# MLP weights loaded 512 columns at a time, four MLP units ahead of the k folds, tile 0 transposed on TensorE, tile 3 not centred first

## Chip, cores, metric

One core of a Trainium2 chip. The metric is device time in microseconds (us) of one execution; most executions of one kernel lie within 0.3%. Ratios of time come with a 95% interval. The profiled span is 1.7 us shorter than the time.

## The reference

`x` is 2048 tokens by 640. After a layer norm, two branches are added to `x`: a linear attention with 32 heads of 20, whose feature maps are softmaxes of `±(q W)` and `±(k W)`, and a gated MLP of width 1536.

```python
xn  = _layernorm(x)
qkv = xn @ wqkv                            # 640 -> 3 * 640
pq, pk = q @ w_phi, k @ w_phi              # per head, 20 x 20
phi = concat(softmax(p), softmax(-p))
o   = (phi_q @ (phi_k^T v)) / (phi_q . sum(phi_k))
out = x + o @ wo + (silu(xn @ w1) * (xn @ w3)) @ w2
```

## The kernel before, where it matters

The kernel lists its operations with what they read and write. A list scheduler inside it, with a model of durations and DMA landings, then puts them into one static order for each engine. A seed shakes the scheduler's choices up to 175 us of its own time.

Tokens come in 16 tiles of 128. The per-head 20x20 matrices are folded into `wqkv` first: a *fold* makes one fifth of the folded weight in 6 matmuls, from block-diagonal `w_phi` (`BDc`) and all five slices of transposed `wqkv` (`wqkT`; each slice is written by one DMA transpose, five for k, five for q). So even the first fold waits for the last slice. A *V tile* or *K tile* multiplies one token tile by the v weights or by the folded weight `Wkp`. An *MLP unit* is 10 matmuls of 512 columns: one chunk of 128 MLP columns for 512 tokens, so it needs tiles 0 to 3 normalised and transposed (`xnT`). An *eviction* is the copy by ACT or DVE that takes a result of TensorE out of its output memory (PS in the rows). *Warm-up matmuls* on constants fill TensorE where it has no work.

A *centred* tile has its mean removed early (`xc`), is transposed by TensorE into `xcT`, and its v tile (`v_first`) needs only that; the scale is applied at eviction. A tile that is not centred waits for the whole norm and takes `v_tile`, from `xnT`.

```python
CENTRED = {0: "ACT", 1: "ACT", 2: "ACT", 3: "DVE"}   # who makes the mean
# ...
TURNED = (0,)                                        # normalised tile transposed by DMA
SEED = 230
# ...
    def load_wT(which, e, level, after=()):          # a DMA transpose of one slice
        return turn(wqkT[:, which * DC + e:which * DC + e + 1, :],
                    A_wqkv[:, which * D + 128 * e:which * D + 128 * e + 128], level, True, after)
# ... the loads of the start; SyncE issues them in the scheduler's order
    n = len(P.all)
    load_w13(0, 384, lv - 4)                         # w1, then w3, columns 0 to 384
    for d in P.all[n:]:
        d.raw.add(chunk)                             # after a piece of wv
    first = [P.all[n]]                               # the w1 piece
    for e in range(DC):
        o = load_wT(1, e, lv - 9 - e, first)         # the k slices wait for it
        if e == 1:
            load(phi_s[:], phi_t, lv - 10.5, "SP", first)
    load_x(4, 8, lv - 19, "SP", [o])                 # waits for the last k slice
    # ...
    load_w13(384, 768, lv - 20)
    load_x(8, 12, lv - 21)
# ...
    for t in range(4):
        if t in CENTRED:
            xc_transpose(t, 6e4 - 10 * t + 15)
        if t in TURNED:
            turn(xnT[:, :, t * 128:(t + 1) * 128], x_tok[:, t, :], 2e6)
        else:
            xn_transpose(t, 3e4 - t if t in CENTRED else 6e4 - 10 * t + 15)
```

The softmax here doesn't subtract the row's maximum and nothing guards it: scores larger than these inputs give would overflow.

Of the kernel before, what the change touches and what calls it, by code (L numbers as in the profile page):

```python
# [4 lines left out]
ACT = mybir.ActivationFunctionType  # L5
# [63 lines left out]
class _Program:  # L69
# [366 lines left out]
    def emit(self, finish):  # L436
# [54 lines left out]
        for o in finish[-4:]:  # L491
            lists["SP"].append(("wait", o.sem[2], o.sem[1]))
        return lists
CENTRED = {0: "ACT", 1: "ACT", 2: "ACT", 3: "DVE"}
POOLED = ()
TURNED = (0,)
SEED = 230
TRIPLES = ((0, 3, 0, 60), (3, 3, 60, 60), (6, 3, 120, 60), (9, 3, 180, 60), (12, 3, 240, 60), (13, 3, 300, 20))


def bass_parallel_sum__linear_kernel_hedgehog__glu_gated_swiglu__prompt_kernel(
# [186 lines left out]
    def load(o, i, level=0.0, eng="SP", after=()):  # L688
        return P.dma(eng, lambda: queue[eng].dma_start(o, i), sb(o), sb(i), *pieces(o, 2 * o.shape[-1]), 0.45, level,  # L689
                     after)  # L690

    def turn(o, i, level=0.0, dram=False, after=()):
        d = P.dma("SP", lambda: nc.sync.dma_start_transpose(o, i), sb(o), sb(i), *pieces(o, 256),  # L693
                  1.31, level, after)
        d.extra = 1.0 if dram else 0.2
        return d
# [10 lines left out]
    def load_x(a, b, level, eng="SP", after=()):  # L707
        return load(x_tok[:, a:b, :], x_t[:, a:b, :], level, eng, after)

    def load_w1(a, b, level, eng="SP"):  # L710
        return load(w1_s[:, :, a:b], w1_t[:, :, a:b], level, eng)

    def load_w3(a, b, level, eng="SP"):
        return load(w3_s[:, :, a:b], w3_t[:, :, a:b], level, eng)

    def load_w13(a, b, level, eng="SP"):
        load_w1(a, b, level, eng)
        load_w3(a, b, level, eng)

    def load_wT(which, e, level, after=()):  # L720
        return turn(wqkT[:, which * DC + e:which * DC + e + 1, :],
                    A_wqkv[:, which * D + 128 * e:which * D + 128 * e + 128], level, True, after)
# [53 lines left out]
    def ln_apply(t, level):  # L776
        o, m, s, z = x_tok[:, t, :], mv[:, t, 0:1], mv[:, t, 4:5], mv[:, t, 6:7]
        ways = [w_op("DVE", "tensor_scalar", (o, o, m, s, ALU.subtract, ALU.mult), 0.35, 0.44)]
        if t in POOLED:
            ways = [w_op("POOL", "tensor_scalar", (o, o, m, s, ALU.subtract, ALU.mult), 2.5, 2.55)]  # L780
        if t >= 4:
            ways.append(w_act(o, o, ACT.Identity, D, s, z))
        add(ways, [o], [o, m, s, z] if t >= 4 else [o, m, s], None, level)

    def centre(t, level, by):
        o, i, z = xc[:, t, :], x_tok[:, t, :], mv[:, t, 6:7]
        if by == "BOTH":
            h, zb = D // 2, mv[:, t, 7:8]
            add([way("ACT", "activation", (junk[:, 0:h], i[:, 0:h], ACT.Copy), dict(scale=-1.0 / D, accum_out=z),
                     0.55, 0.58)], [junk[:, 0:h], z], [i[:, 0:h]], None, level)  # L790
            add([way("DVE", "tensor_scalar", (junk[:, h:D], i[:, h:D], -1.0 / D, None, ALU.mult, ALU.add),
                     dict(accum_out=zb), 0.48, 0.52)], [junk[:, h:D], zb], [i[:, h:D]], None, level)
            add([w_op("DVE", "tensor_scalar", (o, i, z, zb, ALU.add, ALU.add), 0.31, 0.41)], [o], [i, z, zb], None,
                level)
        elif by == "ACT":
            add([way("ACT", "activation", (junk[:], i, ACT.Copy), dict(scale=-1.0 / D, accum_out=z), 0.86, 0.87)],
                [junk[:], z], [i], None, level)
            add([w_op("DVE", "tensor_scalar", (o, i, z, None, ALU.add), 0.31, 0.41),
                 w_act(o, i, ACT.Identity, D, 1.0, z)], [o], [i, z], None, level)
        else:  # L800
            m = mv[:, t, 0:1]
            add([w_op("DVE", "tensor_scalar", (o, i, m, None, ALU.subtract), 0.31, 0.41)], [o], [i, m], None, level)

    def xc_transpose(t, level):
        n = 2 if t == 0 else 1
        u = P.begin(n, level)
        u.name = f"cT{t}"
        for dc in range(DC):
            l = xc[:, t, 128 * dc:128 * dc + 128]
            j, b = (0, dc) if n == 1 or dc < 3 else (1, dc - 3)  # L810

            def emit(l=l, j=j, b=b):
                a = (u.k + j) * 1024 + 128 * b
                return nc.tensor.transpose(PSb[:, a:a + 128], l, ident[:])
            P.mm(emit, [l, ident[:]], j, 0.056, 128)
        for j, a, b in ((0, 0, DC),) if n == 1 else ((0, 0, 3), (1, 3, DC)):
            def src(k, j=j, n=b - a):
                return PSb[:, (k + j) * 1024:(k + j) * 1024 + 128 * n].rearrange("p (c n) -> p c n", n=128)
            o = xcT[:, t, a:b, :]
            add([w_act(o, src, ACT.Copy, 128 * (b - a)), w_copy(o, src, 128 * (b - a), 2)], [o], [], [j], 1e6)  # L820
# [38 lines left out]
    def xn_transpose(t, level):  # L859
        u = P.begin(1, level)  # L860
        u.name = f"xT{t}"
        for dc in range(DC):
            l = x_tok[:, t, 128 * dc:128 * dc + 128]

            def emit(l=l, dc=dc):
                a = u.k * 1024 + 128 * dc
                return nc.tensor.transpose(PSb[:, a:a + 128], l, ident[:])
            P.mm(emit, [l, ident[:]], 0, 0.056, 128)

        def src(k):  # L870
            return PSb[:, k * 1024:k * 1024 + D].rearrange("p (c n) -> p c n", n=128)
        o = xnT[:, :, t * 128:(t + 1) * 128]
        add([w_act(o, src, ACT.Copy, D), w_copy(o, src, D, 2)], [o], [], [0], 1e6)
# [233 lines left out]
    lv = 9e5  # L1107
# [15 lines left out]
    load_wv(4, 5, lv - 3)  # L1123
    on_act(2.65, load_x, 3, 4)
    n = len(P.all)
    load_w13(0, 384, lv - 4)
    for d in P.all[n:]:
        d.raw.add(chunk)
    first = [P.all[n]]
    for e in range(DC):  # L1130
        o = load_wT(1, e, lv - 9 - e, first)
        if e == 1:
            load(phi_s[:], phi_t, lv - 10.5, "SP", first)
    load_x(4, 8, lv - 19, "SP", [o])
    n = len(P.all)
    load_w13(384, 768, lv - 20)
    load_x(8, 12, lv - 21)
    load_w13(768, 1152, lv - 22)
    load_x(12, 16, lv - 23)
    load_w13(1152, 1536, lv - 24)  # L1140
    for e in range(DC):
        load_wT(0, e, lv - 30 - e)
    for d in P.all[n:]:
# [9 lines left out]
    for t in range(4):  # L1153
        if t in CENTRED:
            centre(t, up - t, CENTRED[t])
        ln_apply(t, 1e5 - t)
# [7 lines that stand above are left out]
    for t in range(4, T, 2):  # L1164
# [14 lines left out]
    for t in range(2, 4):  # L1179
        (v_first if t in CENTRED else v_tile)(t, 6e4 - 10 * t)  # L1180
    for dc in range(DC):
# [33 lines left out]

    P.schedule({"PE": 0.8, "ACT": 1.12, "DVE": 0.93, "POOL": 0.8, "SP": 0.81}, filler, 12.0, SEED, 175.0)

# [60 lines left out]
```

## Time and profile before

| | before |
|---|---|
| time, median of 6 runs | 273.77 us (273.62 to 274.39) |
| profiled span, its execution's time | 272.9 us, 274.61 us |
| TensorE busy | 266.8 us, 98% |
| MLP matmuls recorded by the trace / weight loads for them | 465 / 480 |
| issue to landing of a 480 KB piece of w1 or w3, median | 6.8 us |

TensorE is the bound, so the question of each microsecond is whether TensorE does work at its pitch.

### The profile page before, as it was taken

The numbers are of one execution on the slowest core, as the hardware profiler recorded it, in microseconds if no ns is written. First come the engines' busy times: TensorE is split into PE (matmuls) and PEld (weight loads), VectorE is DVE, ScalarE is ACT, GpSimd is POOL, SyncE is SP. The second block draws the span as 40 slices with busy tenths as digits, with TensorE's granted clock in tenths as the row PEclk, the third lists the DMA queues.
The fourth block names the chain that finished last, engine by engine and source line by source line (L and its number), as shares of the span: only waits on it lengthen the run. The fifth ranks groups of instructions, "written<-read, shape, count | busy, mean of one in ns | idle before, by whom it ended". The sixth has DMA issues, their size and how long they took to land.

```text
span 272.9 us, 5057 instructions
## 1 busy us (share of the span) xinstructions
PE 266.8 (98%) x2076; PEld 158.9 (58%) x2095; DVE 181.4 (66%) x324; ACT 103.9 (38%) x194; POOL 61.0 (22%) x101
## 2 busy tenths in 40 slices
PE   8999999999999999999999999999999999999996
PEld 4747447777654446644544446677677774444774
DVE  5756999999998445469789978677661215666112
ACT  6637736777554541255493571010000002222000
POOL 4320643599999800000000000000000000000000
PEclk9999999999999999999999999999999999999999
DMA  7977999773000000712041131343332122000001
GB/s 221 191 98 241 342 221 157 116 168 112 0 0 2 0 0 4 228 62 32 19 50 24 26 49 24 82 113 78 96 98 79 67 73 73 0 0 0 26 24 48
DMA packets 41959, 22.14 MB, mean 81 GB/s; under 512 B 27728, under 2 KB 41936, under 8 KB 41936
## 3 DMA queue, kind: packets, MB, share of 16 engines
q1 hardware_dynamic: 41360, 21.17, 32.9%
q10 hardware_dynamic: 576, 0.66, 0.7%
q8 instruction: 16, 0.26, 0.4%
q14 instruction: 7, 0.06, 0.1%
HBM read 12.81 MB, written 2.62 MB: 57 GB/s over the span
## 4 chain that ended last, share of the span: by engine, by line
PE 82%; DMA 5%; POOL 4%; DVE 3%; SPq 2%; issue 2%; ACT 1%
PE PS L619 82%; POOL ekt L627 3%; SPq L693 2%; DMA w_s<-in_B_w_dram 2%; DMA wv<-in_A_wqkv_dram 1%; DMA wqkT<-in_A_wqkv_dram 1%; ACT EqT L627 1%; POOL mv L627 1%; DVE S L627 1%; DVE v L627 1%; DVE rS L627 1%; SPq L689 0%; DVE x_tok L627 0%; DVE Wqp L627 0%; DVE xres L627 0%
## 5 line engine op out<-in xcount | busy, mean ns | idle before, releaser
L619 PE MATMUL PS<-xnT,w_s 128*128 128x512 bf16 x465 | 105.1, 379 | 1.2 <-issue 0.5
L619 PEld LDWEIGHTS PS<-xnT,w_s 128*128 128x128 bf16 x480 | 46.3, 98 | 54.8 <-issue 0.3
L627 ACT ACTIVATE th<-PS 128x512 f32<-128x512 f32 x48 | 28.6, 597 | 71.2 <-PE PS L619 71.2
L619 PE MATMUL PS<-w_s,hT 128*128 128x320 bf16 (+2 forms) x384 | 55.0, 299 | 0.0
L627 DVE SCALAR_TENSOR_TENSOR t<-th,PS 128x512 bf16<-128x512 f32 x48 | 32.6, 682 | 26.2 <-ACT th L627 26.1
L619 PEld LDWEIGHTS PS<-w_s,hT 128*128 128x128 bf16 x384 | 37.1, 98 | 14.9
L627 DVE TENSOR_TENSOR xres<-PS,xres 128x640 bf16<-128x640 f32 (+2 forms) x17 | 13.4, 786 | 41.0 <-PE PS L619 41.0
L627 POOL TENSOR_TENSOR ekt<-ekt,rS 128x640 bf16<-128x640 bf16 x32 | 39.4, 1265 | 1.1 <-DVE rS L627 1.1
L627 DVE SCALAR_TENSOR_TENSOR hT<-t,PS 128x512 bf16<-128x512 bf16 x48 | 32.5, 680 | 1.1
L627 ACT ACTIVATE EqT<-PS 128x512 bf16<-128x512 f32 x40 | 22.0, 594 | 13.1 <-PE PS L619 13.0
L619 PE MATMUL PS<-wo_s,oT 128*128 128x320 bf16 (+2 forms) x160 | 24.5, 299 | 0.0
L627 DVE TENSOR_TENSOR prod<-PS,g_s 128x1280 bf16<-128x1280 f32 x16 | 23.9, 1491 | 0.5
L619 PE MATMUL PS<-Wkp,xnT 128*128 128x320 bf16 x160 | 23.9, 299 | 0.0
L627 ACT ACTIVATE ekt<-PS 128x640 bf16<-128x640 f32 x32 | 20.7, 699 | 7.4 <-PE PS L619 7.2
L619 PE MATMUL PS<-xnT,Wqp 128*128 128x512 bf16 x96 | 23.0, 379 | 0.4 <-issue 0.3
L627 DVE TENSOR_REDUCE S<-ekt 128x64 f32<-128x1280 bf16 x16 | 22.8, 1452 | 0.0
L627 ACT ACTIVATE e_s<-PS 128x64 f32<-128x64 f32 x32 | 9.1, 284 | 35.2 <-PE PS L619 34.8
L619 PEld LDWEIGHTS PS<-wo_s,oT 128*128 128x128 bf16 x160 | 15.7, 98 | 6.1
L619 PEld LDWEIGHTS PS<-Wkp,xnT 128*128 128x128 bf16 x160 | 15.5, 98 | 5.9 <-ACT Wkp L627 0.2
L619 PE MATMUL PS<-wv,xnT 128*128 128x320 bf16 x120 | 18.3, 299 | 0.0
L627 DVE BATCH_NORM_STATS2 bst<-x_tok 128x6 f32<-128x320 bf16 x32 | 14.3, 469 | 4.2 <-DMA x_tok<-in_A_x_dram 4.2
L619 PEld LDWEIGHTS PS<-xnT,Wqp 128*128 128x128 bf16 x100 | 9.3, 98 | 10.8
(67 smaller groups left out, 168.3 us busy)
## 6 DMA issues: line engine op xcount, KB each, us to landing
w_s<-in_B_w_dram SPq DMA_DIRECT2D x8, 480.0 KB, 6.8
xres<-in_A_x_dram SPq DMA_DIRECT2D x16, 160.0 KB, 2.2
out_dram<-xres SPq DMA_DIRECT2D x15, 160.0 KB, 1.8
x_tok<-in_A_x_dram SPq DMA_DIRECT2D x3, 640.0 KB, 7.6
w_s<-in_B_w_dram SPq DMA_DIRECT2D x1, 1920.0 KB, 9.2
wo_s<-in_A_wo_dram SPq DMA_DIRECT2D x1, 800.0 KB, 5.3
x_tok<-in_A_x_dram SPq DMA_DIRECT2D x2, 160.0 KB, 3.4
x_tok<-in_A_x_dram ACTq DMA_DIRECT2D x2, 160.0 KB, 3.7
```

What stands on the lines that cost most here:

```text
L619: return nc.tensor.matmul(o(u.k), l, r, start=start, stop=stop, skip_group_check=shared)
L627: return getattr(e, name)(*[at(a, u) for a in args], **{k: at(v, u) for k, v in kw.items()})
L693: d = P.dma("SP", lambda: nc.sync.dma_start_transpose(o, i), sb(o), sb(i), *pieces(o, 256), 1.31, level, after)
```

## The change

It means to take away the wait before the k folds: with 512 columns in the first load TensorE has four MLP units to do while the slices of `wqkv` come, and the scheduler is told that these land 2.4 us later than its model says. The other lines rearrange the start around this.

```diff
-CENTRED = {0: "ACT", 1: "ACT", 2: "ACT", 3: "DVE"}
+CENTRED = {0: "ACT", 1: "ACT", 2: "DVE"}
 POOLED = ()
-TURNED = (0,)
-SEED = 230
+TURNED = ()
+SEED = 1138
@@ loads
-    load_w13(0, 384, lv - 4)
+    load_w13(0, 512, lv - 4)
@@ k slices
         o = load_wT(1, e, lv - 9 - e, first)
+        o.extra = 2.4
@@ later loads
-    load_w13(384, 768, lv - 20)
+    load_w13(512, 1024, lv - 20)
     load_x(8, 12, lv - 21)
-    load_w13(768, 1152, lv - 22)
+    load_w13(1024, 1536, lv - 22)
     load_x(12, 16, lv - 23)
-    load_w13(1152, 1536, lv - 24)
```

## The prediction

> **What bounds the kernel now.** I read the page first (busy shares and the 40 slices), then TensorE's order of work in time, then who waits for whom, then the chain of waits, and last the issues of single DMAs in the first 30 us, because the diff touches only that stretch and the order that the kernel's own list scheduler makes of it.
>
> The page's first two parts, busy time (share, instructions) and busy tenths:
>
> ```profile
> PE 266.8 (98%) x2076; PEld 158.9 (58%) x2095; DVE 181.4 (66%) x324; ACT 103.9 (38%) x194; POOL 61.0 (22%) x101
> ...
> PE   8999999999999999999999999999999999999996
> ...
> PEclk9999999999999999999999999999999999999999
> ```
>
> TensorE (PE) is the bound, at full clock. A busy PE is not yet a PE at its pitch, so I count real work by start times. TensorE's rows in time (start, length, operation, count):
>
> ```profile
> 4.54 0.44 PE L814 MATMUL PS<-ident,xc 128*128 128x128 bf16 x5
> 4.82 0.45 PE L1098 MATMUL PS<-const-bfloat16-1.0 128*128 128x128 bf16 x5
> 5.57 0.99 PE L619 MATMUL PS<-wv,xcT 128*128 128x320 bf16 x6 [0.29 <-ACT xcT L627]
> ...
> 10.54 0.44 PE L814 MATMUL PS<-ident,xc 128*128 128x128 bf16 x5
> 10.82 1.00 PE L867 MATMUL PS<-ident,x_tok 128*128 128x128 bf16 x15
> 11.66 1.52 PE L619 MATMUL PS<-wv,xcT 128*128 128x320 bf16 x10
> 13.39 6.42 PE L619 MATMUL PS<-xnT,w_s 128*128 128x512 bf16 x29 [0.21 <-issue]
> 19.81 0.41 PE L619 MATMUL PS<-BDc,wqkT 128*128 128x80 bf16 x2
> 20.93 1.48 PE L619 MATMUL PS<-BDc,wqkT 128*128 128x140 bf16 x25 [0.71 <-DMA wqkT<-in_A_wqkv_dram]
> 22.25 5.60 PE L619 MATMUL PS<-Wkp,xnT 128*128 128x320 bf16 x40
> 27.90 12.90 PE L619 MATMUL PS<-xnT,w_s 128*128 128x512 bf16 x58
> ```
>
> The first useful matmul (transposes of centred token tile 0) starts at 4.54; then V of tiles 0 to 3, three MLP units (10 matmuls of 512 columns each), a pause of 0.71 for the last transposed slice of wqkv, the five folds, K of tiles 0 to 3, and MLP again at 27.90. Pitches from the same view: an MLP unit is 2.14 to 2.16 us (two start 2.16 apart at 74.52 and 76.68; twelve lie between 226.06 and 251.74, 25.68/12 = 2.14), a V or K tile 1.36 (40.63 to 41.99), five 128-column transposes 0.28 (10.54 to 10.82).
>
> Work between 4.54 and 27.90, in us: 35 transposes x 0.056 = 1.96; 4 V tiles x 1.36 = 5.44; 3 MLP units x 2.155 = 6.47; 30 fold matmuls at about 0.053 = 1.60; 4 K tiles x 1.36 = 5.44. Sum 20.9, in 23.36 us: **2.45 us of slack**, and this is all that the change can win there. It lies so: 1.1 before 10.54 (15 transposes and three V tiles, 4.9, in 6.0 us; warm-up matmuls 0.45, a wait of 0.29, small ones), 0.37 before the first MLP unit (10.54 to 13.39 is 2.85 for 20 transposes and one V tile, 2.48), 0.71 before the folds, 0.25 in small pieces.
>
> After 27.90 there is almost none. From 27.90 to 106.47 (the start of the kv sums) I count 18 MLP units, 24 V and K tiles, 5 Q units of 1.08 and 30 fold matmuls: 38.8 + 32.6 + 5.4 + 1.6 = 78.4 of 78.57 us. The end, 226.06 on, is matmuls at pitch to 270.39 and a fixed tail of addition and store, 2.5 us. TensorE's waits, all of them above 0.2 us in sum:
>
> ```profile
> PE PS L619 <- issue: 0.8, 5, 0.2
> PE PS L1098 <- PEq L1263: 0.8, 1, 0.8
> PE PS L619 <- DMA wqkT<-in_A_wqkv_dram: 0.7, 1, 0.7
> PE PS L619 <- ACT xcT L627: 0.3, 1, 0.3
> ```
>
> The long waits of the other engines and POOL's full slices 7 to 13 cost nothing: no row of TensorE names them.
>
> The start of the chain of waits shows why the folds come at 20.93:
>
> ```profile
> 5.16 5.61 DMA w_s<-in_B_w_dram
> 10.77 0.02 issue
> 10.79 1.17 SPq L693
> ...
> 17.27 3.53 DMA wqkT<-in_A_wqkv_dram
> ```
>
> SyncE starts the five DMA transposes of wqkv when the first w1 piece has landed (10.77), issues them one by one at 1.2 to 2.0 us each, with the small phi load between, and the last lands at 20.80.
>
> **What the Trainium skill says.** (1) "TensorE: Matmul & The Clock Gate", section "Wait — 56ns, not 53.3ns?": warm matmuls run at N / 2.4 GHz plus about 2.5 ns, 55.6 ns at 128 columns and 215.7 at 512. The trace agrees: 15 transposes in 0.84 us are 56 ns each, and an MLP unit of ten is 2.14 to 2.16 us. (2) "VectorE: DVE Perf Modes", section "The three transpose paths": TensorE transposes 128x128 in 390 ns into PSUM, the DMA in 1309 ns. In this kernel, pipelined, five TensorE transposes take 0.28 us plus an eviction of 0.49 (DVE) or 0.70 (ACT), while tile 0's DMA transpose was issued at 6.30 and took 6.6 us to land. (3) "DMA: Bandwidth & Descriptors", section "Bandwidth": larger transfers come nearer the peak, at least 1 MiB being advised. The loads grow from 480 to 640 KB, so I give this little; the trace moves 334 to 355 GB/s between 24 and 30 us already.
>
> **The change part by part.**
> *Tile 0 on TensorE.* Adds 5 transposes (0.28 us) and an eviction; removes a DMA transpose, 1.30 us on SyncE's queue and a landing at 6.30 + 6.6 = 12.9. This landing stands right at the end of V3 (11.66 + 1.36 = 13.0), so I suspect it behind the 0.37 before the first MLP unit. Without it that unit can start when the TensorE transposes are evicted: those of tiles 1 to 3 were all out at 12.35.
> *Tile 3 not centred.* Removes 5 transposes (0.28), the centring (0.38) and an eviction (0.49) on DVE. TensorE's sum of work is unchanged: 35 transposes either way. But V3 now needs the normalised, transposed tile like the MLP, so 1.36 us of work that filled 11.66 to 13.02 is no longer early. Before the first MLP unit there are 35 x 0.056 + 3 x 1.36 = 6.0 us of work; with 1.1 slack TensorE would be through at 11.7, and must wait for the last eviction, at about 12.2. V3 then goes anywhere later. Slack before the first MLP unit: 12.2 - 4.54 - 6.0 = 1.6, against 1.1 + 0.37 = 1.5. Loss 0.1 to 0.2.
> *Tile 2 centred by its mean from DVE.* Takes 0.74 + 0.19 off ACT and waits for two statistics and an aggregate (0.44 + 0.48 + 0.21 = 1.1), so its centred form is some 0.2 later; V1 covers that.
> *Loads of 512 columns.* w1 lands when 0.164 MB more has passed: at about 340 GB/s 0.5 us later, 11.25; w3, issued at 5.62 and landed 6.6 later by the list of single issues, near 12.2, comes at about 13.1. The second half of the first unit needs w3 1.08 after its start: 13.3. Just in time. The transposes of wqkv start 0.5 later, but no transpose of tile 0 stands before them; the last lands near 21.1.
> *Four units ahead of the folds.* The units run 12.2 to 20.8; with V3 (1.36) TensorE has work to 22.2, past 21.1. The 0.71 is gone. Folds and K take 7.0, so MLP resumes near 29.2. It then needs columns 512 to 1024. Before, that stretch's w1 and w3 were issued at 21.23 and about 21.8 and took 5.4 and 6.4, landing at 26.6 and 28.2; with 0.16 and 0.33 MB more and a start 0.3 later, 27.4 and 29.5, needed at 29.2 and 30.3. No wait expected.
> *Seed and the model's 2.4 us extra for those landings.* They move no work, only the order up to 175 us. Gaps from mode switches (five of 0.16 in the rows above) and evictions may change by 0.3 either way.
> Sum: -0.71 + 0.15 + 0 = about -0.55; 273.8 becomes 273.2.
>
> **The rivals.**
> *The new wait takes the old one's place:* w1 or w3 late by more than reckoned holds the first unit, or columns 512 to 1024 hold the unit after K. For it: margins of 0.2 to 1.8 us. Against: the pauses would be under 1 us, and V3 or another unit can be put in. Time 273.6 to 274.5.
> *The start fills better than I think:* ACT and DVE lose tile 3's early steps, the tiles are out by 11.7, and most of the 2.45 goes. Against: the input of tile 3 and its statistics (aggregated at 9.35 to 9.56, power on POOL to 10.60, scaled by 11.1) do not move. Time 272.0 to 272.6.
> *The folds were not worth waiting for at all:* the pause vanishes but the new seed gives the 0.5 back between 106 and 167 us, where softmax steps on DVE and ACT gate the token units. Time 273.5 to 274.
> A wait of many us would need the order to be badly off, and nothing in a stretch with 78.4 of 78.57 us filled suggests it.
>
> **Range and chances.** Predicted 273.2; 272.1 to 274.4 covers all three rivals. Two per cent is 5.5 us, over twice the slack that the change can touch (2.45), so faster by that is all but excluded; slower by that needs a stall that nothing shows. Faster 0.02, within 0.96, slower 0.02.
>
> **What would show it right or wrong.** Right: no wait of TensorE for wqkT; 40 MLP matmuls between V and the folds; folds beginning at 21 to 22.3; K of tiles 0 to 3 ending some 1.6 us later than 27.85 with one unit more done; the first MLP unit at 12 to 12.6 with no DMA wait; 78.5 us at pitch after. Wrong: a row of TensorE waiting for w_s (loads too big), for x_tok or xnT before 13 us for over 1 us (tile 3 too late), or a rise of the waits for DVE after 106 us (seed).

## More of the kernel before

The prediction shows TensorE's rows of the start. One line that I passed over belongs beside them, from the page's list of groups (count, then busy time and mean of one, then idle time before):

```profile
L619 PE MATMUL PS<-xnT,w_s 128*128 128x512 bf16 x465 | 105.1, 379 | 1.2 <-issue 0.5
L619 PEld LDWEIGHTS PS<-xnT,w_s 128*128 128x128 bf16 x480 | 46.3, 98 | 54.8 <-issue 0.3
```

There are 480 weight loads and 465 matmuls: 15 records of matmuls are missing. Where the missing one is the first of a row, the row shows 9 or 29 matmuls and seems to start 0.216 us late, behind a gap.

## The result, and the profile after

After: 273.35 us, median of 6 runs (273.20 to 274.27), against 273.77; ratio 0.9988, interval 0.9971 to 1.0005: the same, with a lean to faster. A ratio compares the means, so it is not quite the ratio of the medians quoted. Executions over 1.5% slower than the fastest of the same kernel are left out of the means.

The profiled span fell from 272.9 to 271.7. That is 1.2 us, more than the 0.42 of the medians, because the profiled execution of before was a slow one (274.61, above all six timed runs). The trace of before shows more to explain than there is.

TensorE's rows of the start of the kernel after:

```profile
4.63 0.74 PE L814 MATMUL PS<-ident,xc 128*128 128x128 bf16 x5
5.17 0.60 PE L1098 MATMUL PS<-const-bfloat16-1.0 128*128 128x128 bf16 x5
...
10.92 1.29 PE L867 MATMUL PS<-ident,x_tok 128*128 128x128 bf16 x20
12.05 1.52 PE L619 MATMUL PS<-wv,xnT 128*128 128x320 bf16 x10
13.40 8.80 PE L619 MATMUL PS<-xnT,w_s 128*128 128x512 bf16 x40
22.04 1.82 PE L619 MATMUL PS<-BDc,wqkT 128*128 128x140 bf16 x30
23.70 5.67 PE L619 MATMUL PS<-Wkp,xnT 128*128 128x320 bf16 x40
29.21 13.11 PE L619 MATMUL PS<-xnT,w_s 128*128 128x512 bf16 x60
```

All 40 matmuls of the four units are there, the folds follow at 22.04 with nothing between, and MLP resumes at 29.21. TensorE waits for nothing that the view of waits names, but its first instruction:

```profile
PE PS L1098 <- PEq L1263: 0.8, 1, 0.8
```

SyncE's issues in the kernel after (start, time on the queue) show when the slices come:

```profile
11.73 3.00 SPq L693 DMA_TRANSPOSE wqkT<-in_A_wqkv_dram  x2
...
15.40 3.83 SPq L693 DMA_TRANSPOSE wqkT<-in_A_wqkv_dram  x3
20.93 0.37 SPq L689 DMA_DIRECT2D x_tok<-in_A_x_dram  x1
```

The load of x at 20.93 waits for the last slice, so its start tells the landing: 20.9, no earlier than before (20.8), and 1.1 before TensorE reaches the folds.

For all traces I split the time at the V of tile 4, which every order puts behind K of tiles 0 to 3. The **start** is that moment less 2.158 us for each MLP unit already done (twelve units lie in 25.90 us, 224.68 to 250.58, in the trace after, where all 120 are recorded). The **rest** is the beginning of the last addition less the start. Before: V of tile 4 at 40.63 with 9 units done, so the start is 21.22 (with 2.157, as I used it below), and the last addition at 270.42 makes the rest 249.20. After: 42.16 with 10 units, 20.59, and 269.25, 248.66. So 0.6 us of the trace's difference are in the start and 0.5 in the rest.

One place of the rest is visible: the second and third q fold. Before took 0.90 us for these 12 matmuls (the next row starts at 66.30), as the second half of the second fold waited for the eviction of the first fold on DVE; after took 0.63 (66.92 to 67.55). Before:

```profile
65.28 0.48 DVE L627 CAST Wqp<-PS 128x320 bf16<-128x320 f32 x1
65.40 1.06 PE L619 MATMUL PS<-BDc,wqkT 128*128 128x140 bf16 x12
65.81 0.47 PEld L619 LDWEIGHTS PS<-BDc,wqkT 128*128 128x128 bf16 x9 [0.25 <-DVE Wqp L627]
```

### The profile page after: what moved, and what is told of

It reads as the page before. It is cut to its first block, busy times and chain, and to the rows that moved or that the text cites. A ratio compares the mean times of both kernels' runs of the same rounds, so it can differ in the third digit from the quotient of the medians.

```text
span 271.7 us, 5074 instructions
## 1 busy us (share of the span) xinstructions
PE 268.3 (99%) x2098; PEld 159.4 (59%) x2098; DVE 182.5 (67%) x325; ACT 101.8 (37%) x190; POOL 60.8 (22%) x101
## 4 chain that ended last, share of the span: by engine, by line
PE 99%; DVE 0%; issue 0%
PE PS L619 96%; PE PS L1098 2%; PE PS L867 0%; PE PS L814 0%; DVE xres L627 0%
## 5 line engine op out<-in xcount | busy, mean ns | idle before, releaser
L619 PE MATMUL PS<-xnT,w_s 128*128 128x512 bf16 x480 | 106.6, 379 | 0.0
L627 ACT ACTIVATE ekt<-PS 128x640 bf16<-128x640 f32 x32 | 20.8, 701 | 9.0 <-PE PS L619 8.8
L619 PE MATMUL PS<-wv,xnT 128*128 128x320 bf16 x130 | 19.8, 299 | 0.0
```

What stands on the lines that cost most here:

```text
L619: return nc.tensor.matmul(o(u.k), l, r, start=start, stop=stop, skip_group_check=shared)
L627: return getattr(e, name)(*[at(a, u) for a in args], **{k: at(v, u) for k, v in kw.items()})
```

## The experiments

Each kernel in 6 executions (5 rounds and the profiled one), compared with the kernel before on the same chip. The landing is that of the last k slice, read from SyncE's next load. The start and the rest are as defined above. These columns come from one profiled execution each.

| run | median us | ratio (95%) | landing | folds from | waits for wqkT | start | rest |
|---|---|---|---|---|---|---|---|
| before, first trace | 273.77 | 1 | 20.8 | 19.65 | 0.71 | 21.22 | 249.20 |
| a1_same | 274.04 | 0.9994 (0.998 to 1.0009) | 19.1 | 19.84 | 0 | 20.51 | 249.07 |
| a4_seed | 274.71 | 1.0015 (1.0002 to 1.0028) | 21.0 | 20.24 | 0.45 | 21.56 | 248.81 |
| b4_noextra | 274.10 | 0.9991 (0.9978 to 1.0003) | 20.1 | 19.90 | 0 | 20.46 | 248.73 |
| a3_tiles | 275.56 | 1.0054 (1.0036 to 1.0071) | 19.3 | 18.84 | 0.18 | 21.88 | 249.26 |
| after, first trace | 273.35 | 0.9988 (0.9971 to 1.0005) | 20.9 | 22.04 | 0 | 20.59 | 248.66 |
| c1_after | 273.72 | 0.9988 (0.9971 to 1.0006) | 21.2 | 21.91 | 0 | 20.46 | 248.66 |
| c2_latehalf | 274.00 | 1.0004 (0.998 to 1.0028) | 20.6 | 20.00 | 0.34 | 21.05 | 248.89 |
| d1_before_late | 275.06 | 1.004 (1.0015 to 1.0064) | 21.6 | 20.25 | 0.88 | 22.00 | 249.08 |
| d2_after_late | 274.55 | 1.0022 (1.0002 to 1.0042) | 22.0 | 22.74 | 0 | 21.28 | 249.45 |
| a2_loads | 274.98 | 1.0036 (1.0016 to 1.0056) | 20.5 | 21.08 | 0 | 21.63 | 248.90 |
| b1_allbutseed | 275.32 | 1.005 (1.0031 to 1.0069) | 19.5 | 21.15 | 0 | 21.80 | 248.81 |
| b2_turn0 | 274.92 | 1.0038 (1.0011 to 1.0065) | 21.0 | 22.63 | 0 | 21.18 | 248.74 |
| c4_afterfold | 273.68 | 0.9997 (0.9975 to 1.0018) | 19.3 | 21.80 | 0 | 20.35 | 248.73 |

The theory going in: the gain is the wait of 0.71, less a small loss at the start. The rivals: the seed's other order after 40 us makes it, or it is chance.

**a1_same.** No edit: the kernel before a second time.

> The kernel before, unchanged, run as if it were a new one: how far apart are two readings of the same program? My theory (the gain of 0.4 us is the removed wait for wqkT of 0.7, less what the start loses) expects a ratio of 1.000 within 0.001 and a second trace with the same wait for wqkT, 0.5 to 0.9 us, before the folds. The rival (the 0.4 us is the spread of the runs) expects two readings of one program to differ by 0.4 us or more.

The ratio is 1 within its interval, as both expected of a mean, but the wait is not there. TensorE's rows of this trace:

```profile
12.00 1.52 PE L619 MATMUL PS<-wv,xcT 128*128 128x320 bf16 x10
13.58 6.42 PE L619 MATMUL PS<-xnT,w_s 128*128 128x512 bf16 x29
19.84 1.86 PE L619 MATMUL PS<-BDc,wqkT 128*128 128x140 bf16 x30
21.54 5.60 PE L619 MATMUL PS<-Wkp,xnT 128*128 128x320 bf16 x40
```

The slices landed at 19.1, 1.7 us earlier than in the first trace, and the folds ran through. Of this, 1.1 was there when the slices set out: SyncE starts them when the first w1 piece has landed, at 10.79 in the first trace and at 9.73 here. One program in two executions: a start of 21.22 and one of 20.51. This half of my theory fell: the 0.71 was this execution's, not the kernel's.

**a4_seed.** The kernel before with `SEED = 1138`.

> The kernel before with the new seed alone. Its order is that of before up to the folds and differs after 30 us. My theory: the wait for wqkT stays at 0.5 to 0.9 us and the time at 273.6 to 274.0, ratio 0.999 to 1.001. The rival (the new order after 40 us makes the gain): the time falls to about 273.3, ratio 0.998 to 0.999, with the wait for wqkT still there.

Neither: it is slower, ratio 1.0015 (interval from 1.0002). The rest is 0.3 shorter than before's, as the rival wanted, but the seed also moved tile 0's DMA transpose behind the first slice of `wqkv` on SyncE's queue (issued at 11.02 instead of 6.30), and the first MLP unit waited for it:

```profile
13.99 6.42 PE L619 MATMUL PS<-xnT,w_s 128*128 128x512 bf16 x29 [0.33 <-DMA xnT<-x_tok]
21.11 1.57 PE L619 MATMUL PS<-BDc,wqkT 128*128 128x140 bf16 x25 [0.45 <-DMA wqkT<-in_A_wqkv_dram]
```

Here the DMA transpose of tile 0 is seen on the path, by name.

**b4_noextra.** The kernel after less one line:

```diff
         o = load_wT(1, e, lv - 9 - e, first)
-        o.extra = 2.4
```

> The kernel after without the 2.4 us that its scheduler adds to the landings of the transposed slices: the loads stay at 512 columns, but only three MLP units stand ahead of the first folds and the fourth comes between folds. My theory: TensorE waits again for wqkT, 0.5 to 1.3 us in sum, and the time is 273.8 to 274.5, ratio to before 1.000 to 1.003. The rival (seed or loads make the gain): as after, 273.3, ratio 0.998 to 0.999.

The order was as described: three units, three folds, the fourth unit, two folds. The wait did not come, and the ratio is that of after:

```profile
19.90 1.12 PE L619 MATMUL PS<-BDc,wqkT 128*128 128x140 bf16 x18
20.86 2.32 PE L619 MATMUL PS<-xnT,w_s 128*128 128x512 bf16 x9
23.02 0.79 PE L619 MATMUL PS<-BDc,wqkT 128*128 128x140 bf16 x12
```

My theory's number missed. The slices landed near 20.1, about when the first fold needed the last of them. So the place of the fourth unit alone is worth nothing measurable in a run where the slices are on time.

**a3_tiles.** The first two lines of the diff alone (`CENTRED`, `TURNED`).

> The kernel before with the tile part alone (tile 0 transposed on TensorE, tile 2 centred by DVE's mean, tile 3 not centred); loads of 384 columns, old seed. The scheduler then sets two MLP units ahead of the folds and the third behind them. My theory: TensorE reaches the folds near 18 us and waits there until wqkT lands at about 20, 1.5 to 2.5 us, so 275.0 to 276.0, ratio 1.004 to 1.008. A rival (the start matters little, since work moves freely) expects under 0.5 us of loss, ratio below 1.002.

The time fits, the reason doesn't: the wait for wqkT was 0.18. The loss lies ahead of the first unit, which starts at 14.5:

```profile
9.54 0.98 PE L1098 MATMUL PS<-const-bfloat16-1.0 128*128 128x128 bf16 x14
...
13.15 1.53 PE L619 MATMUL PS<-wv,xnT 128*128 128x320 bf16 x10 [0.42 <-DVE xnT L627]
```

With tile 3 no longer centred TensorE ran short of work, 14 warm-up matmuls filled in, and V of tile 3 waited for its transposed tile.

From here the theory was: the start of after is no better than before's good start, but cannot become before's bad one, since the fourth unit covers a late landing; and the rest is about 0.4 shorter.

**c1_after.** The kernel after again.

> The kernel after, unchanged, a second reading on another chip. By the traces so far, the time up to the V of tile 4 less 2.157 us for each MLP unit done by then is 21.22 and 20.51 for two traces of before and 20.59 for after; the rest is 249.20 and 249.07 for before and 248.66 for after. My revised theory: the rest is smaller by 0.4 us in every trace with the new seed, and the start is no better than before's good trace, but cannot have before's bad one, since the fourth unit covers a landing of wqkT up to about 22 us. So again a ratio of 0.997 to 0.999, a start of 20.4 to 20.8, a rest of 248.6 to 248.9, and no wait of TensorE for wqkT. The rival (the first comparison was chance): ratio 0.999 to 1.001 and a rest of 249 or more.

As expected on every count: ratio 0.9988, start 20.46, rest 248.66, no wait for wqkT although the slices landed at 21.2, later than in any trace of before with its own loads. The two readings together (their mean, the half-width of 0.0017 divided by the root of 2) give 0.9988 with an interval of about 0.9976 to 1.0000. Each reading alone includes 1.

**c2_latehalf.** The kernel before, whose scheduler changes to the new seed at 45 us:

```diff
         while left:
+            if seed is not None and seed > 0 and free["PE"] > 45.0:
+                rng, seed = random.Random(1138), -1
             best = None
```

> The kernel before with its own order up to 45 us of the scheduler's time and the new seed from there on; loads, tiles and the start untouched. My revised theory: the rest after the V of tile 4 falls from 249.1 to 248.6 to 248.8, the ratio is 0.998 to 0.9995, and the start has before's spread (20.5 to 21.3). The rival (the rest differs for another reason than the later order, for instance the loads): rest 249.0 to 249.3, ratio 1.000.

The trace's rest fell by 0.2 to 0.3, to 248.89 (just above what I expected), and the q folds no longer wait (0.63 for the 12 matmuls), but the timed ratio, 1.0004 with an interval of ±0.0024, can't show a gain of this size. The same program start as before gave a third value of the wait, 0.34, at a landing of 20.6. It also shows a second gap, ahead of the first unit:

```profile
13.74 6.42 PE L621 MATMUL PS<-xnT,w_s 128*128 128x512 bf16 x29 [0.54 <-issue]
```

With the missing record the unit starts at 13.53, 0.48 after V of tile 3 is through (13.05); tile 0's DMA transpose landed at 13.1 (issued at 6.52, 6.6 to landing). The landing accounts for the beginning of this gap; what held TensorE for the rest of it the trace does not name.

**d1_before_late, d2_after_late.** The same line in before and after makes the k slices wait for the w3 piece instead of w1:

```diff
-    first = [P.all[n]]
+    first = [P.all[n + 1]]
```

> The kernel before with the transposed loads of wqkv started when the first w3 piece has landed instead of the first w1 piece, so some 1.4 us later (w3 landed 1.4 after w1 in the trace of before); TensorE's order is the same up to the V of tile 4. My theory: before has no cover, so the wait for wqkT before the folds grows to 1.5 to 2.2 us and the time by 0.8 to 1.6 us, ratio 1.003 to 1.006. The rival (the wait is absorbed elsewhere or not on the path): ratio below 1.002.

> The same delay in the kernel after: the transposed loads of wqkv start when the first w3 piece of 512 columns has landed, some 1.5 to 1.9 us later, with TensorE's order unchanged through the folds. wqkT landed at 20.9 in the trace of after and is needed at 22.04, so my theory lets the fourth unit absorb 1.1 us of the delay: a wait for wqkT of 0.3 to 0.9 us and a time 0.3 to 1.0 above that of after, about equal to before, ratio 0.999 to 1.002. The rival (no cover): it loses the full 1.5 or more, ratio 1.003 or more.

The delay brings before waits of 0.18 and 0.70 (0.88; I had expected 1.5 or more) and 1.1 us of time:

```profile
20.79 0.22 PE L619 MATMUL PS<-BDc,wqkT 128*128 128x140 bf16 x1 [0.18 <-DMA wqkT<-in_A_wqkv_dram]
21.71 1.48 PE L619 MATMUL PS<-BDc,wqkT 128*128 128x140 bf16 x25 [0.70 <-DMA wqkT<-in_A_wqkv_dram]
```

In after the slices landed latest of all traces, 22.0, and no wait followed, where I had expected 0.3 to 0.9:

```profile
14.32 8.58 PE L619 MATMUL PS<-xnT,w_s 128*128 128x512 bf16 x39
22.74 1.82 PE L619 MATMUL PS<-BDc,wqkT 128*128 128x140 bf16 x30
```

So the cover is shown in the traces: TensorE reached the folds 0.7 later than in after, but even at after's 22.04 the last slice would have been in. In the times it is not clear of noise, as the intervals of d1 and d2 overlap. What I had not expected is that d2 still lost time without this wait (ratio 1.0022, just above my range). In its trace TensorE waited 0.40 for the centred tile 2 ahead of 9.15, so that everything behind came later, and the rest is 249.45 with another order after 45 us, in which an MLP unit at 142.43 waits 0.47 for an eviction on DVE. Neither is a wait for wqkT. Whether the delayed transposes have any part in them stays open.

**a2_loads.** The load lines and the 2.4 us alone, on the kernel before.

> The kernel before with the loads of 512 columns and the scheduler's 2.4 us alone; tile 0 still transposed by DMA, tile 3 still centred, old seed. Its scheduler puts three units, then four of five folds, a fourth unit and the last fold. My theory: the DMA transpose of tile 0 stands behind 1.3 MB of weights instead of 0.98, so the first MLP unit waits for it, 0.4 to 1.0 us, and the time up to the V of tile 4 less the units done is 21.2 to 21.9; the rest 249.0 to 249.3; ratio 1.001 to 1.004. The rival (the loads and the fourth unit carry the gain by themselves): ratio 0.997 to 0.999.

Ratio and start came in as my theory had them, and the rival fell. The wait, however, is put down to another:

```profile
13.57 0.44 PE L867 MATMUL PS<-ident,x_tok 128*128 128x128 bf16 x5
14.82 6.42 PE L619 MATMUL PS<-xnT,w_s 128*128 128x512 bf16 x29 [0.81 <-DVE xnT L627]
```

The DMA transpose of tile 0 (issued at 6.59, 6.7 to landing) was in at 13.2. The scheduler, presumably reckoning with a late landing, had put one tile's TensorE transposes behind V of tile 3, and their eviction (14.05 to 14.54 on DVE) held the unit. So this order cost more than a wait for the DMA transpose would have.

**b1_allbutseed.** The kernel after with `SEED = 230`.

> The kernel after with the old seed. The old seed puts the transposes of tiles 0 to 3 in another order: V of tile 2 is left in front of the transposes of tiles 1 to 3, and TensorE runs 14 warm-up matmuls and waits for tile 3. My theory: the first MLP unit starts near 14.5 (a gap of 0.4 to 0.8 us before V of tile 3, as in the run of the tile part alone), start 21.2 to 21.8, rest 248.7 to 249.3, ratio 1.000 to 1.003. The rival (the seed matters only after 40 us): start 20.4 to 20.8, ratio 0.999 to 1.0005.

As my theory had it for the trace (14 warm-up matmuls again, 0.43 before V of tile 3, start 21.80), with a loss above its range, 1.005. The seed is no ornament: with these tiles it decides whether the start fills. The rest, 248.81 with the old seed, also shows that the shorter rest does not belong to the number 1138.

**b2_turn0.** The kernel after with `TURNED = (0,)`.

> The kernel after with tile 0 transposed by DMA again. My theory: that transpose stands behind the two loads of 640 KB and lands at 13.5 to 14.2, so the first MLP unit waits for it by 0.3 to 0.9 us; start 20.9 to 21.5, rest 248.6 to 248.9, ratio 1.000 to 1.002. The rival (the DMA transpose was never on the path): start as after, 20.4 to 20.8, ratio 0.998 to 0.999.

```profile
11.83 1.53 PE L619 MATMUL PS<-wv,xnT 128*128 128x320 bf16 x10
14.22 8.58 PE L619 MATMUL PS<-xnT,w_s 128*128 128x512 bf16 x39 [0.86 <-ACT v L627]
```

One record is missing here (39, and 22.63 less 40 matmuls of 0.2158 is 14.00), so the unit started at 14.0, 0.8 after V of tile 3 was through (11.83 + 1.36 = 13.19). The profile names the eviction of v on ACT, but that ended at 14.11, after the start; the DMA transpose landed at 13.9 (issued at 11.18, 2.7 to landing). That transpose is the release that fits. The start lost 0.6 to 0.7 against after. The time lost 0.5% against it (1.0038 / 0.9988), more than I had expected and twice what this trace shows: its execution was the fastest of six, three of which took 274.1 to 274.4 and three 275.4 to 276.0. What the slower three lost has no trace.

**c4_afterfold.** The kernel after, the q folds' evictions at a higher level (the scheduler's priority):

```diff
-            add([w_act(...), w_copy(o, src, 320)], [o], [], [q], 1e6)
+            add([w_act(...), w_copy(o, src, 320)], [o], [], [q], 1e6 if which else 2e6)
```

> An attempt to beat both: the kernel after with the evictions of the q folds given a higher level in the scheduler, so that no fold waits for one (in before one of them waited 0.27 us; in after none does). If nothing is left to win there, as I think: start 20.4 to 20.8, rest 248.6 to 248.9, ratio 0.997 to 0.9995, as after. The rival (evictions of the folds still cost something): rest below 248.4.

Start 20.35, rest 248.73: as after, and the ratio 0.9997, a little above what I expected, is not told apart from after's. No gain is seen there; no version beats after. Its slices landed at 19.3 with after's loads.

## Why the prediction was right

The time predicted was 273.2, the time measured 273.35 and, in the second reading, 273.72, inside 272.1 to 274.4; the class is the same, as given 0.96. Point by point:

- **"about -0.55", sum:** measured -0.42 in the medians, -0.26 in the second reading. The size fits, its make-up only in part: the wait was on average worth less than I took, the loss ahead of the first unit is not there, and a gain in the rest that I had not forecast is. So the hit on the size is in part luck.
- **"-0.71", the wait for wqkT:** gone in all traces of after (landings 20.9 and 21.2, folds at 22.04 and 21.91). But the term was mis-sized: with before's own start the wait was 0.71, 0 and 0.34 in three traces, 0.35 on average. (Counted from the first fold to K of tile 0, which leaves modelled ends of matmuls out, it is 2.60, 1.70 and 2.07 against 1.66 in after: the wait cost 0.9, 0 and 0.4.) I read one execution as the kernel. What the change removes is an exposure to a landing that moves by 1.7 us between executions.
- **"Loss 0.1 to 0.2" ahead of the first unit:** not shown. I had the unit at 12.2 with V of tile 3 afterwards; it came at 13.40, right behind V of tile 3 (12.05 + 1.36 = 13.41). From the first useful matmul to the first unit, each corrected where its first record is missing, the first traces give 8.77 after (13.40 - 4.63) and 8.63 before (13.17 - 4.54), which looks like the forecast loss. But c1_after has 8.64, and before has 8.73 in a1_same and 8.79 in c2_latehalf: no difference that one can tell.
- **"I suspect it behind the 0.37":** right in the mechanism, wrong in the size. With the missing record (29 of 30) the gap was 0.16. In the trace's records of semaphores TensorE's queue stands at the wait for tile 0's DMA transpose, which landed at 12.93; the unit's first weight load went out at 13.15, 0.26 after the last matmul of V of tile 3 had started. In a1_same the transpose landed at 11.9 (6.47 + 5.4), that load went out together with that matmul, and there was no gap. Where it landed at 13.1 (c2_latehalf) the gap was 0.48. So before has two exposures to a landing that moves, and the change removes both; a4_seed shows this second wait by name, b2_turn0 by its times.
- **"Gaps from mode switches (five of 0.16 in the rows above)":** four of the five were not gaps, and the fifth is the one just named. Each stood before a row with a record missing; the trace of after, with all 480, shows none. For the same reason the 2.14 per unit was 2.16, and the slack of 2.45 up to 27.90 was 2.2. The row of two fold matmuls at 19.81 is the end of a row of five from 19.65, cut off by its view's window.
- **"Folds and K take 7.0, so MLP resumes near 29.2 ... No wait expected":** 29.21, and no wait for w_s. "the last lands near 21.1": 20.9 and 21.2, but with the same first loads 19.3 in c4_afterfold and 20.1 in b4_noextra, so a hit this close is partly luck.
- **"They move no work, only the order", ±0.3:** half right. The rest fell by 0.4 to 0.5 in the traces. Taken from start to start of TensorE's matmuls, 0.26 of it is the eviction that the second q fold waited for, and 0.15 lies in two rows of attention matmuls of before (KVc, at 123.61 and 143.37) that begin 0.17 us after the pitch of the row ahead of them is through, where all such rows of after take 0.10. The first trace of before alone lost another 0.10, within the kv sums at 111.0. As to the seed, it decides the start as well: without it the change is 0.5% slower than before.
- **The range:** held, and neither a late weight nor a late tile 3 showed. But three of the change's parts alone lose, 0.54% (tiles), 0.36% (loads and 2.4 us), 0.15% (seed). I treated the parts as terms of a sum. They are one package, because each one alone leads the scheduler to an order that runs TensorE dry ahead of the first unit (a3_tiles) or leaves it waiting there for one tile's transposed form (a2_loads, a4_seed).

Not settled: whether the gain of 0.1% is real (two readings of 0.9988, each with 1 in its interval, while the same kernel read twice gave 0.9994).

## What to carry to other kernels

A wait of a few tenths in one trace may belong to that execution: before a change is aimed at it, profile the same program twice and see whether the landing moves. Whether cover for a DMA that lands at varying times works is seen by delaying the DMA on purpose, even where the median shows little. In a kernel whose order comes from a scheduler, test the parts of a change apart: a part that is harmless by count may still give an order that is not.

## What the Trainium skill lacked or had wrong

- "DMA: Bandwidth & Descriptors", section "Bandwidth", gives one time per size; how much a landing moves between executions of one program it doesn't say. Here the last of five DMA transposes landed at 20.8, 20.6 and 19.1 us with the same loads and order on SyncE's queue ahead of them.
- "TensorE: Matmul & The Clock Gate", section "What's actually happening", has the warm-up end at a moment that varies by ±500 ns. The traces agree: the five transposes of tile 0 start 56 ns apart in the first trace of before (4.54 to 4.82) and 108 ns apart in that of after (4.63 to 5.17), at the same place in the program; in a1_same, the kernel before again, they look like after's. The page sets the penalty below 1%; here the 0.3 us between the two rows are 0.1% of the span, as much as the change gained. Whether they reach the end of the kernel no run shows.
- None of the pages drawn on here warns that a missing matmul record looks like a gap. Here 15 of 480 were missing, seven of them the first of a row. Three of these stand in the rows as gaps of 0.16 to 0.21 us with "issue" as their cause, and only at one of the three, 13.39, was there a real wait (0.16).
- "VectorE: DVE Perf Modes", section "The three transpose paths", has 1309 ns for a DMA transpose of 128x128. A tile of five such blocks took 1.30 us on SyncE's queue alone, and 6.6 us to landing behind two weight loads, 2.7 us in b2_turn0, where it was issued at 11.18.
